# Batch 0 of a fused cosFormer attention and MLP kernel: row sums of k by a selector weight, fewer idle matmuls, another order of chunk 0, two pieces of q on GpSimd

## The chip, the cores and the metric

The kernel runs on one core of a Trainium2 chip. The metric is the device time of one execution in microseconds (us). All times below that carry a decimal point and no other unit are microseconds from the start of the profiled span.

## The reference, cut to what matters

q, k and v are [8 batches, 8 heads, 576 positions, 64], the weights are w_in [512, 2048] and w_out [2048, 512], all float32.

```python
def phi(x, c, s):                       # c, s: cos and sin of pi/2 * position / 576
    r = np.maximum(x, 0.0)
    return np.concatenate([r * c, r * s], axis=-1)      # 64 -> 128 features
q_p, k_p = phi(q, cos_w, sin_w), phi(k, cos_w, sin_w)
kv  = np.einsum('bhsf,bhsd->bhfd', k_p, v)
z   = np.sum(k_p, axis=2)
num = np.einsum('bhsf,bhfd->bhsd', q_p, kv)
den = np.einsum('bhsf,bhf->bhs', q_p, z)[..., None] + 1e-06
x   = (num / den).transpose(0, 2, 1, 3).reshape(8 * 576, 512)
h   = x @ w_in
out = (h * (1.0 / (1.0 + np.exp(-1.702 * h)))) @ w_out
```

## The kernel before, in words

The batches are worked one after the other. Of each batch, the attention part gives x, four chunks of 128 rows and a tail of 64; `mm1` multiplies x by w_in in 16 column blocks (fc) of 128, `gelu` evacuates each block on ScalarE (ACT), and `mm2` multiplies by w_out. The attention work of the next batch is spread between the `mm2` calls of the batch at hand. Batch 0 has no batch before it, so its attention part stands alone at the start, and this is the part that the change touches.

The program is written in a fixed order (`tc.manual_schedule()`): each engine works through its own instructions in the order in which the calls stand in the text, and waits where an operand isn't ready. The tiles of the two PSUM pools (`pmm`, four buffers named mm; `pat`, two buffers named at) are handed out again when the last reader of a buffer is done; a new tile takes the buffer whose release comes first in the program.

Batch 0 goes like this:

- SyncE (SP) loads k and q as float32 in two cuts each. GpSimd (POOL) waits for the first piece of k (`gate`, L141), then issues the two halves of v as bfloat16 (`vb`, L143), then blocks 0 to 3 and 4 to 7 of w_in (`load_win`, L122), and after a second gate that waits for the end of v (L146) the rest of w_in and the loads of batch 1.
- `idle` (L387) gives TensorE (PE) matmuls on zeros until k is there: 12 of 512 columns and 48 of 64.
- `trig` (L156 on ACT, L158 on VectorE, DVE) makes the features of k (`kr`) and q (`qn`), position piece j of 9 at a time, a cosine and a sine instruction each.
- `ksum` (L235) sums k's features over the positions: for each of four head pairs i and nine pieces j a matmul with `kr[:, j, i, :]` as the weight and the two columns of `sel` as the moving operand, 36 in all; a DVE copy (L237) puts them as column 64 into `kvs`.
- `qturn_pe` (L191) transposes q's features, two pieces j at a time, and `qevac` (L201 on DVE, L199 on ACT) copies them to `qT`.
- `kv_mm` (L223) makes k'v for head pairs 0 and 1 from v's first half, then for pairs 2 and 3 from the second; `kv_evac` (L228) copies each to `kvs`.
- `num_halves` (L247 to L257) makes numerator, denominator and quotient of chunk 0 in two halves of four heads; `x_half` (L265, L267) turns each into `xT`. Chunks 1 to 3 take `num_mm` (L274), `num_div` (L282 to L286), `xturn_mm` (L303) and `xturn_evac` (L310, ACT).
- `x_part(c)` (L326) multiplies chunk c by blocks fc 0 to 3 of w_in: 4 fc by 4 pieces kc of the contraction, 16 matmuls of 128 columns. Chunk 0 is cut in two calls (fc 0 and 1, then 2 and 3), and the transposes of chunk 1 stand between them; those of chunk 2 stand ahead of `x_part(1)`, those of chunk 3 ahead of `x_part(2)`.
- `gelu` (L331) then evacuates the four blocks, and `mm1` of fc 4 and later follow with 512 columns each.

Of the kernel before, what the change touches and what calls it, by code (L numbers as in the profile page):

```python
# [9 lines left out]
F32 = mybir.dt.float32  # L10
BF16 = mybir.dt.bfloat16
AF = mybir.ActivationFunctionType
MUL = mybir.AluOpType.mult
ADD = mybir.AluOpType.add
MAX = mybir.AluOpType.max
# [4 lines left out]
def kernel(  # L20
# [9 lines left out]
    nc = tc.nc  # L30
    B, H, S, D = q.shape
    d_model = H * D
    d_ff = moe_w_in.shape[1]
    KC = d_model // 128
    FC = d_ff // 128
    NS = S // 64
    MT = 512
# [7 lines left out]
    small = ctx.enter_context(tc.tile_pool(name="small", bufs=3))  # L45
    pmm = ctx.enter_context(tc.tile_pool(name="pmm", bufs=4, space=PSUM))
# [12 lines left out]
    kf, vf, vb = raw("kf"), raw("vf"), raw("vb", BF16)  # L59
    qf0 = qf[:, 0:NI * S].rearrange("p (i e) -> p i e", i=NI)  # L60
# [10 lines left out]
    ident = const.tile([128, 128], BF16)  # L71
# [3 lines left out]
    warm = const.tile([128, 512], BF16)  # L75
# [10 lines left out]
    sel = const.tile([128, 2], BF16)  # L86
# [9 lines left out]
    kr = one.tile([128, NS, NI, 128], BF16, name="kr")  # L96
# [4 lines left out]
    qT = one.tile([128, H, 640], BF16, name="qT")  # L101
# [18 lines left out]
    def load_win(i, f0):  # L120
        n = w_in_t[i].shape[2]
        nc.gpsimd.dma_start(out=w_in_t[i], in_=win_r[:, :, f0:f0 + n])  # L122

    def wcol(kc, fc):

        g, c = divmod(fc, 4)
        w = w_in_t[g][:, kc, :] if g < 2 else w_in_t[2][:, kc, ts(g - 2, 512)]
        return w.rearrange("p (f c) -> p f c", c=4)[:, :, c]
# [14 lines left out]
        nc.gpsimd.dma_start(out=vb[:, i:i + 2], in_=src_of(v, 0, i, i + 2))  # L143
    load_win(0, 0)
    load_win(1, 512)
    nc.gpsimd.tensor_copy(gate[0:1, 1:2], vb[0:1, 3, 0:1])  # L146
    load_win(2, 1024)


    def trig(dst, src, j, act=False):  # L150

        i = src[:, :, ts(j, 64)]
        for cs, w in enumerate((cosw, sinw)):
            o = dst[:, j, :, ts(cs, 64)]
            if act is True or (act == "sin" and cs == 1):
                nc.scalar.activation(o, i, AF.Relu, scale=w[:, j:j + 1])  # L156
            else:
                nc.vector.tensor_scalar(o, i, 0.0, w[:, j:j + 1], op0=MAX, op1=MUL)  # L158

    def trig_q(c, act=False):  # L160
        n = 128 if c < 4 else 64
# [21 lines left out]
    def qturn_pe(c, at=False):  # L183
        if at:
            tp = pat.tile([128, 2, 512], F32, name="at")[:, 0].bitcast(BF16).rearrange(
                "p (j i t) -> p j i t", j=2, i=NI)
        else:
            tp = pmm.tile([128, 2, NI, 128], BF16, name="mm")
        for j in range(2 * c, min(2 * c + 2, NS)):
            for i in range(NI):  # L190
                nc.tensor.transpose(tp[:, j % 2, i], qn0[:, j, i, :], ident)  # L191
        tps[c] = tp

    def qevac(c, act=False):
        n = min(2 * c + 2, NS) - 2 * c
        o = qT[:, :, ds(c * 128, n * 64)].rearrange("f h (j p) -> f j h p", j=n)
        i = tps[c][:, 0:n].rearrange("f j i (hh p) -> f j (i hh) p", hh=2)
        if act:
            nc.scalar.activation(o, i, AF.Copy)  # L199
        else:  # L200
            nc.vector.tensor_copy(o, i)  # L201
# [6 lines left out]
    st = {}  # L208

    def kv_open(i0=0, i1=NI, n=65):  # L210
        t = pat.tile([128, 2, 512], F32, name="at")
        for i in range(i0, i1):
            st["kv", i] = t[:, :, ds((i - i0) * n, n)]
        st["ps", i0] = t[:, :, 0:(i1 - i0) * n]
        if i0 == 0:
            st["kvs"] = small.tile([128, 2, NI, VW], BF16, name="kvs", bufs=2)

    def kv_mm(i0, i1, rhs, col, n):
        for i in range(i0, i1):
            for j in range(NS):  # L220
                for hh in range(2):
                    r = slice(hh * 64, hh * 64 + 64)
                    nc.tensor.matmul(st["kv", i][:, hh, ds(col, n)], kr[r, j, i, :], rhs(r, i, j),  # L223
                                     start=(j == 0), stop=(j == NS - 1))

    def kv_evac(i0, i1, n=65):
        o = st["kvs"][:, :, i0:i1, 0:n]
        nc.vector.tensor_copy(o, st["ps", i0].rearrange("p hh (i e) -> p hh i e", e=n))  # L228

    def ksum():  # L230

        t = pmm.tile([128, 512], F32, name="mm")
        for i in range(NI):
            for j in range(NS):
                nc.tensor.matmul(t[:, ts(i, 2)], kr[:, j, i, :], sel,  # L235
                                 start=(j == 0), stop=(j == NS - 1))
        nc.vector.tensor_copy(st["kvs"][:, :, :, 64].rearrange("p hh i -> p i hh"),  # L237
                              t[:, 0:8].rearrange("p (i hh) -> p i hh", hh=2))

    nums = {}  # L240


    def num_halves():
        ps = [pmm.tile([128, 512], F32, name="mm") for _ in range(2)]
        for h in range(H):
            i, hh = divmod(h, 2)
            nc.tensor.matmul(ps[h // 4][:, ds((h % 4) * 65, 65)], qT[:, h, 0:128],  # L247
                             st["kvs"][:, hh, i, 0:65], start=True, stop=True)
        pv = [p[:, 0:260].rearrange("p (h e) -> p h e", h=4) for p in ps]
        den = small.tile([128, 2, 4], F32, name="den")  # L250
        for a in range(2):
            nc.vector.tensor_scalar(den[:, a], pv[a][:, :, 64], 1e-6, None, op0=ADD)
        inv = small.tile([128, 2, 4], F32, name="inv")
        nc.vector.reciprocal(inv, den)
        for a in range(2):
            xn = small.tile([128, 4, 64], BF16, name="xh")
            nc.vector.tensor_tensor(xn, pv[a][:, :, 0:64],  # L257
                                    inv[:, a].unsqueeze(2).to_broadcast([128, 4, 64]), op=MUL)
            nums[0, a] = [ps[a], xn]

    def x_half(b, a):
        ps, xn = nums.pop((0, a))
        o = ps[:, 264:392].bitcast(BF16)
        for k in range(2):
            nc.tensor.transpose(o[:, ts(k, 128)], xn.rearrange("p h e -> p (h e)")[:, ts(k, 128)],  # L265
                                ident)
        nc.scalar.activation(x_cols(b, 0)[:, 2 * a:2 * a + 2], o.rearrange("p (k t) -> p k t", k=2),  # L267
                             AF.Copy)
# [9 lines left out]
    def num_div(c):  # L278
        ps = nums[c][0]
        pv = ps[:, :, 0:260].rearrange("p a (h e) -> p a h e", h=4)  # L280
        den = small.tile([128, 2, 4], F32, name="den")
        nc.vector.tensor_scalar(den, pv[:, :, :, 64], 1e-6, None, op0=ADD)  # L282
        inv = small.tile([128, 2, 4], F32, name="inv")
        nc.vector.reciprocal(inv, den)
        xn = small.tile([128, 2, 4, 64], BF16, name="xn", bufs=4)
        nc.vector.tensor_tensor(xn, pv[:, :, :, 0:64],  # L286
                                inv.unsqueeze(3).to_broadcast([128, 2, 4, 64]), op=MUL)
        nums[c].append(xn)
# [3 lines left out]
    def x_open(b):  # L292
        x[b] = xpool.tile([128, KC, MT], BF16, name="xT")
# [4 lines left out]
    def xturn_mm(c):  # L298
        ps, xn = nums[c]
        xv = xn.rearrange("p a h e -> p (a h e)")  # L300
        for kc in range(KC):
            o = ps[:, kc // 2, ds(264 + (kc % 2) * 64, 64)].bitcast(BF16)
            nc.tensor.transpose(o, xv[:, ts(kc, 128)], ident)  # L303
# [80 lines left out]
    def idle(n, cols=512):  # L384
        w = pmm.tile([128, 512], F32, name="mm")
        for _ in range(n):
            nc.tensor.matmul(w[:, 0:cols], warm[:, 0:128], warm[:, 0:cols], start=True, stop=True)  # L387
# [26 lines left out]
        xturn_evac(b, 4)  # L414


    idle(12)
    idle(48, 64)
    for j in (0, 1):
        trig(kr, kf, j)  # L420
    trig(kr, kf, 2, act=True)
# [2 lines left out]
    trig(kr, kf, 6, act="sin")  # L424
    for j in (7, 8):
        trig(kr, kf, j, act=True)
    kv_open(0, 2, 64)
    kv_open(2, 4, 64)
    for j in (0, 1):
        trig(qn0, qf0, j)  # L430
    for j in (2, 3):
        trig(qn0, qf0, j, act=True)
    ksum()
    qturn_pe(0)
    qevac(0)
    qturn_pe(1)
    qevac(1)
    for j in (4, 5, 7):
        trig(qn0, qf0, j, act=True)
    trig(qn0, qf0, 6)  # L440
    kv_mm(0, 2, vb_rhs, 0, 64)
    kv_evac(0, 2, 64)
    qturn_pe(2)
    qevac(2, act=True)
    kv_mm(2, 4, vb_rhs, 0, 64)
    kv_evac(2, 4, 64)
    qturn_pe(3)
    qevac(3, act=True)
    x_open(0)
    num_halves()  # L450
    num_mm(1)
    num_div(1)
    x_half(0, 0)
    x_half(0, 1)
    num_mm(2)
    num_div(2)

    def x_part(c, f0=0, f1=4):
        for fc in range(f0, f1):
            mm1_part(0, fc, c * 128, c * 128 + 128)  # L460

    x_part(0, 0, 2)
    xturn_mm(1)
    xturn_evac(0, 1)
    x_part(0, 2, 4)
    num_mm(3)
    num_div(3)
    xturn_mm(2)
    xturn_evac(0, 2)
    x_part(1)  # L470
    xturn_mm(3)
    xturn_evac(0, 3)
    trig(qn0, qf0, 8)
    x_part(2)
    x_part(3)
    for fc in range(4):
        gelu(fc)
# [144 lines left out]
```

## Time and profile before

| what | value |
|---|---|
| time, median of 3 runs (lowest to highest) | 292.13 us (291.91 to 292.35) |
| the profiled execution: its own time, and its span | 292.35 us, 290.6 us |
| PE busy | 283.8 us, 98% of the span |
| ACT, DVE, POOL busy | 128.0, 124.4, 56.4 us |
| granted TensorE clock | 0.999 |

The span runs from the first to the last instruction; the execution's own time has 1.75 us more around it. "Busy" of PE counts a matmul until its result is in PSUM, so that a stream of short matmuls is busy without a gap while its starts are some 56 ns apart. In the chain of work that ended last each piece stands at the time when it became what everything later waited for; in the timeline each piece stands at its first start.

### The profile page before, as it was taken

What the parts mean: (1) busy time and instruction counts of PE and PEld (TensorE: products, weight loads), DVE (VectorE), ACT (ScalarE), POOL (GpSimd) and SP (SyncE); (2) the same over time, 40 slices, a digit from 0 to 9 for tenths busy, and PEclk for the clock granted to TensorE, in tenths of its full rate; (3) what the DMA queues carried; (4) which work ended last, traced back from release to release, by engine and by line L of the source; (5) the groups of instructions that cost most, each with busy time, mean ns of one, the idle gap of its engine ahead of it and who ended that gap; (6) DMA issues with size and microseconds to landing.
All of it is one profiled execution on the core that took longest, in us unless ns stands there. A gap on an engine that the chain in (4) does not pass through costs nothing.

```text
span 290.6 us, 5918 instructions
## 1 busy us (share of the span) xinstructions
PE 283.8 (98%) x2396; PEld 156.1 (54%) x2396; DVE 124.4 (43%) x360; ACT 128.0 (44%) x223; POOL 56.4 (19%) x60
## 2 busy tenths in 40 slices
PE   8889999999999999999999999999999999999995
PEld 3775646855545554555455545554555455554444
DVE  4856514872695248615950587048804300000000
ACT  6957733662147213641265116601671156751111
POOL 6332003200055013601250016001600100001000
PEclk9999999999999999999999999999999999999999
DMA  7999999999999998897799479958901410002322
GB/s 246 245 219 290 350 167 228 356 243 237 283 282 219 333 187 184 181 379 157 158 202 398 112 149 165 392 167 119 186 13 55 107 68 1 0 2 45 84 88 74
DMA packets 73211, 53.54 MB, mean 184 GB/s; under 512 B 52608, under 2 KB 62592, under 8 KB 73184
## 3 DMA queue, kind: packets, MB, share of 16 engines
q1 hardware_dynamic: 67216, 37.24, 54.7%
q0 software_dynamic: 5968, 15.93, 20.5%
q8 instruction: 19, 0.31, 0.4%
q14 instruction: 8, 0.07, 0.1%
HBM read 36.70 MB, written 9.44 MB: 159 GB/s over the span
## 4 chain that ended last, share of the span: by engine, by line
PE 91%; DMA 6%; DVE 1%; ACT 0%; POOL 0%; issue 0%; ACTq 0%
PE mm L375 41%; PE mm L326 38%; PE mm L354 4%; PE at L223 3%; PE at L274 3%; DMA vb<-in_v_dram 2%; DMA xT<-xn 2%; DMA kf<-in_k_dram 1%; PE mm L347 1%; PE at L303 1%; POOL vb L143 0%; PE mm L191 0%; DVE xn L286 0%; ACT xT L310 0%; PE mm L265 0%
## 5 line engine op out<-in xcount | busy, mean ns | idle before, releaser
L375 PE MATMUL mm<-w_out_sb,g 128*128 128x512 bf16 (+1 forms) x528 | 117.4, 373 | 0.0
L326 PE MATMUL mm<-xT,w_in 128*128 128x512 bf16 (+1 forms) x608 | 114.1, 345 | 0.4 <-ACT xT L267 0.2
L331 ACT ACTIVATE g<-mm 128x512 bf16<-128x512 f32 x128 | 75.6, 598 | 33.0 <-PE mm L326 33.0
L326 PEld LDWEIGHTS <-w_in 128*128 128x128 bf16 x608 | 61.4, 113 | 49.7 <-issue 0.6
L382 POOL DMA_DIRECT2D out_dram<-ysb x34 | 45.5, 1339 | 195.6 <-ACT ysb L379 195.5
L375 PEld LDWEIGHTS <-g 128*128 128x128 bf16 x528 | 48.8, 98 | 50.0
L379 ACT ACTIVATE ysb<-mm 128x512 f32<-128x512 f32 (+1 forms) x37 | 21.7, 586 | 115.6 <-PE mm L375 115.6
L286 DVE TENSOR_TENSOR xn<-at,inv 128x512 bf16<-128x512 f32 x39 | 27.0, 691 | 4.0 <-DMA xT<-xn 2.7
L228 DVE CAST kvs<-at 128x520 bf16<-128x520 f32 (+1 forms) x9 | 5.8, 640 | 53.2 <-PE at L223 53.2
L158 DVE TENSOR_SCALAR kr<-kf,cosw 128x256 bf16<-128x256 f32 x69 | 24.2, 351 | 6.0 <-DMA kf<-in_k_dram 6.0
L158 DVE TENSOR_SCALAR kr<-kf,sinw 128x256 bf16<-128x256 f32 x68 | 23.2, 341 | 0.0
L282 DVE TENSOR_SCALAR den<-at 128x8 f32<-128x8 f32 x39 | 6.5, 166 | 32.1 <-PE at L274 32.1
L274 PEld LDWEIGHTS <-qT 128*128 128x128 bf16 x312 | 14.2, 97 | 7.7 <-issue 0.6
L171 DVE TENSOR_SCALAR qn<-qf,cosw 128x512 bf16<-128x512 f32 (+1 forms) x33 | 15.8, 478 | 3.2 <-DMA qf<-in_q_dram 3.2
L171 DVE TENSOR_SCALAR qn<-qf,sinw 128x512 bf16<-128x512 f32 (+1 forms) x33 | 15.8, 478 | 0.0
L274 PE MATMUL at<-kvs,qT 128*128 128x65 bf16 x312 | 15.5, 193 | 0.2 <-ACT xT L310 0.2
L375 PE MATMUL mm<-w_out_sb,gt 128*128 128x512 bf16 x64 | 14.0, 379 | 0.0
L354 PE MATMUL mm<-xt,w_in 128*128 128x448 bf16 x64 | 12.3, 352 | 0.0
L223 PEld LDWEIGHTS <-kr 64*128 64x128 bf16 x576 | 9.3, 94 | 3.3 <-issue 2.9
L375 PEld LDWEIGHTS <-gt 128*128 128x128 bf16 x64 | 6.3, 98 | 7.5
L356 ACT ACTIVATE gt<-mm 128x448 bf16<-128x448 f32 x16 | 8.7, 544 | 3.3 <-PE mm L354 3.2
L354 PEld LDWEIGHTS <-w_in 128*128 128x128 bf16 x64 | 7.3, 114 | 4.9
(69 smaller groups left out, 99.7 us busy)
## 6 DMA issues: line engine op xcount, KB each, us to landing
kf<-in_k_dram SPq DMA_DIRECT2D x6, 1152.0 KB, 10.3
vf<-in_v_dram SPq DMA_DIRECT2D x6, 1152.0 KB, 11.7
qf<-in_q_dram SPq DMA_DIRECT2D x6, 1024.0 KB, 6.0
out_dram<-ysb POOLq DMA_DIRECT2D x24, 256.0 KB, 4.3
w_out_sb<-in_moe_w_out_dram POOLq DMA_DIRECT2D x4, 512.0 KB, 17.1
out_dram<-ysb POOLq DMA_DIRECT2D x10, 128.0 KB, 7.4
kf<-in_k_dram POOLq DMA_DIRECT2D x1, 1152.0 KB, 13.0
vf<-in_v_dram POOLq DMA_DIRECT2D x1, 1152.0 KB, 15.8
```

Of the source, the lines that this page charges most:

```text
L158: nc.vector.tensor_scalar(o, i, 0.0, w[:, j:j + 1], op0=MAX, op1=MUL)
L171: nc.vector.tensor_scalar(o, i, 0.0, sc, op0=MAX, op1=MUL)
L223: nc.tensor.matmul(st["kv", i][:, hh, ds(col, n)], kr[r, j, i, :], rhs(r, i, j), start=(j == 0), stop=(j == NS - 1))
L274: nc.tensor.matmul(ps[:, h // 4, ds((h % 4) * 65, 65)], qT[:, h, ts(c, 128)], st["kvs"][:, hh, i, 0:65], start=True, stop=True)
L286: nc.vector.tensor_tensor(xn, pv[:, :, :, 0:64], inv.unsqueeze(3).to_broadcast([128, 2, 4, 64]), op=MUL)
L326: nc.tensor.matmul(hp[fc][:, t0:t1], wcol(kc, fc), x[b][:, kc, t0:t1], start=(kc == 0), stop=(kc == KC - 1))
L331: nc.scalar.activation(g, hp.pop(fc), AF.Gelu_apprx_sigmoid)
L354: nc.tensor.matmul(hps[:, 64:B * 64], wcol(kc, fc), xt[:, kc, 64:B * 64], start=(kc == 0), stop=(kc == KC - 1))
L356: nc.scalar.activation(gt[:, fc, 64:B * 64], hps[:, 64:B * 64], AF.Gelu_apprx_sigmoid)
L375: nc.tensor.matmul(yp[b, t, c0][:, c0:c1], w, w_out_sb[:, fc, c0:c1], start=(fc == 0), stop=(fc == FC - 1))
L379: nc.scalar.activation(ysb[:, c0:c1], yp[b, t, c0][:, c0:c1], AF.Identity)
L382: eng.dma_start(out=dst[:, c0:c1], in_=ysb[p0:p0 + n, c0:c1])
```

## The change

- The 60 idle matmuls become 9 of 512 columns. Five more stand between the matmuls of the sums.
- The sums of k take `sel` as the weight and a whole piece `kr[:, j]` (512 columns) as the moving operand: 9 matmuls (`ksum_mm`) into rows 0 and 1 of one tile, in the order in which the pieces become ready. A DVE copy of [2, 512] takes the rows to SBUF (`ksum_rows`), four matmuls against a 2 by 2 identity turn them into columns (`ksum_turn`), and the old DVE copy puts them into `kvs`.
- Pieces 6 and 8 of q go from DVE to GpSimd, ahead of the gate and of the load of the last part of w_in, which move behind them in POOL's queue. Pieces 4, 5 and 7 stay on ACT and move ahead in the text.
- Chunk 0's numerator and quotient for heads 0 to 3 (`num_half(0)`, `div_half(0)`) stand ahead of `kv_mm(2, 4)`, and `x_half(0, 0)` stands between `kv_evac(2, 4)` and `qturn_pe(3)`. The other half follows `qturn_pe(3)`.
- `x_part(0)` is one block of 16 matmuls, the contraction's first two pieces for all four fc, and then the last two. The transposes of chunk 1 stand behind all of it, those of chunk 2 behind `x_part(1)`, and those of chunk 3 behind `x_part(2)`.

```diff
-    nc.gpsimd.tensor_copy(gate[0:1, 1:2], vb[0:1, 3, 0:1])
-    load_win(2, 1024)
...
-    def ksum():
-
-        t = pmm.tile([128, 512], F32, name="mm")
+    def ksum_mm(j, first=False, last=False):
+
+        if first:
+            st["ks"] = pmm.tile([128, 512], F32, name="mm")
+        nc.tensor.matmul(st["ks"][0:2], sel, kr[:, j].rearrange("p i f -> p (i f)"),
+                         start=first, stop=last)
+
+    def ksum_rows():
+        st["row"] = small.tile([2, 512], BF16, name="row", bufs=1)
+        nc.vector.tensor_copy(st["row"], st["ks"][0:2])
+
+    def ksum_turn():
         for i in range(NI):
-            for j in range(NS):
-                nc.tensor.matmul(t[:, ts(i, 2)], kr[:, j, i, :], sel,
-                                 start=(j == 0), stop=(j == NS - 1))
+            nc.tensor.matmul(st["ks"][:, ts(i, 2)], st["row"][:, ts(i, 128)], ident[0:2, 0:2],
+                             start=True, stop=True)
...
-    idle(12)
-    idle(48, 64)
+    idle(9)
...
+    for n, j in ((0, 0), (0, 2), (0, 1), (4, 3), (0, 7), (1, 4), (1, 8), (0, 5), (0, 6)):
+        if n:
+            for _ in range(n):
+                nc.tensor.matmul(spare, warm[:, 0:128], warm, start=True, stop=True)
+        ksum_mm(j, first=(j == 0), last=(j == 6))
+        if j == 0:
+            spare = pmm.tile([128, 512], F32, name="mm")
     kv_open(0, 2, 64)
     kv_open(2, 4, 64)
     for j in (0, 1):
         trig(qn0, qf0, j)
-    for j in (2, 3):
+    for j in (2, 3, 4, 5, 7):
         trig(qn0, qf0, j, act=True)
-    ksum()
+    for j in (6, 8):
+        trig(qn0, qf0, j, eng=nc.gpsimd)
+    nc.gpsimd.tensor_copy(gate[0:1, 1:2], vb[0:1, 3, 0:1])
+    load_win(2, 1024)
+    ksum_rows()
     qturn_pe(0)
     qevac(0)
     qturn_pe(1)
     qevac(1)
-    for j in (4, 5, 7):
-        trig(qn0, qf0, j, act=True)
-    trig(qn0, qf0, 6)
+    ksum_turn()
     kv_mm(0, 2, vb_rhs, 0, 64)
     kv_evac(0, 2, 64)
     qturn_pe(2)
     qevac(2, act=True)
+    num_half_open()
+    num_half(0)
+    div_half(0)
+    x_open(0)
     kv_mm(2, 4, vb_rhs, 0, 64)
     kv_evac(2, 4, 64)
+    x_half(0, 0)
     qturn_pe(3)
     qevac(3, act=True)
-    x_open(0)
-    num_halves()
+    num_half(1)
+    div_half(1)
     num_mm(1)
     num_div(1)
-    x_half(0, 0)
     x_half(0, 1)
     num_mm(2)
     num_div(2)
...
-    x_part(0, 0, 2)
+    for fc in (0, 1, 3, 2):
+        hp[fc] = pmm.tile([128, MT], F32, name="mm")
+    for k0 in (0, 2):
+        for fc in range(4):
+            for kc in (k0, k0 + 1):
+                nc.tensor.matmul(hp[fc][:, 0:128], wcol(kc, fc), x[0][:, kc, 0:128],
+                                 start=(kc == 0), stop=(kc == KC - 1))
     xturn_mm(1)
     xturn_evac(0, 1)
-    x_part(0, 2, 4)
     num_mm(3)
     num_div(3)
+    x_part(1)
     xturn_mm(2)
     xturn_evac(0, 2)
-    x_part(1)
+    x_part(2)
     xturn_mm(3)
     xturn_evac(0, 3)
-    trig(qn0, qf0, 8)
-    x_part(2)
     x_part(3)
```

`num_half(a)` and `div_half(a)` do for half a what `num_halves` did for both, with a reciprocal of four columns for each half.

More of the change, by code (lines that the diff above doesn't have):

```diff
@@ L145, with trig @@
     load_win(1, 512)
-    nc.gpsimd.tensor_copy(gate[0:1, 1:2], vb[0:1, 3, 0:1])
-    load_win(2, 1024)
-    def trig(dst, src, j, act=False):
+    def trig(dst, src, j, act=False, eng=nc.vector):
         i = src[:, :, ts(j, 64)]
@@ L157, in trig @@
             else:
-                nc.vector.tensor_scalar(o, i, 0.0, w[:, j:j + 1], op0=MAX, op1=MUL)
+                eng.tensor_scalar(o, i, 0.0, w[:, j:j + 1], op0=MAX, op1=MUL)
     def trig_q(c, act=False):
@@ L233, in ksum @@
+    def ksum_turn():
         for i in range(NI):
-            for j in range(NS):
-                nc.tensor.matmul(t[:, ts(i, 2)], kr[:, j, i, :], sel,
-                                 start=(j == 0), stop=(j == NS - 1))
+            nc.tensor.matmul(st["ks"][:, ts(i, 2)], st["row"][:, ts(i, 128)], ident[0:2, 0:2],
+                             start=True, stop=True)
         nc.vector.tensor_copy(st["kvs"][:, :, :, 64].rearrange("p hh i -> p i hh"),
-                              t[:, 0:8].rearrange("p (i hh) -> p i hh", hh=2))
+                              st["ks"][:, 0:8].rearrange("p (i hh) -> p i hh", hh=2))
@@ L240, with num_half_open, num_half @@
     nums = {}
-    def num_halves():
-        ps = [pmm.tile([128, 512], F32, name="mm") for _ in range(2)]
-        for h in range(H):
+    def num_half_open():
+        nums["ps"] = [pmm.tile([128, 512], F32, name="mm") for _ in range(2)]
+    def num_half(a):
+        ps = nums["ps"][a]
+        for h in range(4 * a, 4 * a + 4):
             i, hh = divmod(h, 2)
-            nc.tensor.matmul(ps[h // 4][:, ds((h % 4) * 65, 65)], qT[:, h, 0:128],
+            nc.tensor.matmul(ps[:, ds((h % 4) * 65, 65)], qT[:, h, 0:128],
@@ L248, in num_halves, with div_half @@
                              st["kvs"][:, hh, i, 0:65], start=True, stop=True)
[L249 to L253, printed above, removed]
-        nc.vector.reciprocal(inv, den)
[L255 to L259, printed above, removed]
+    def div_half(a):
+        pv = nums["ps"][a][:, 0:260].rearrange("p (h e) -> p h e", h=4)
+        den = small.tile([128, 4], F32, name="denh")
+        nc.vector.tensor_scalar(den, pv[:, :, 64], 1e-6, None, op0=ADD)
+        inv = small.tile([128, 4], F32, name="invh")
+        nc.vector.reciprocal(inv, den)
+        xn = small.tile([128, 4, 64], BF16, name="xh")
+        nc.vector.tensor_tensor(xn, pv[:, :, 0:64],
+                                inv.unsqueeze(2).to_broadcast([128, 4, 64]), op=MUL)
+        nums[0, a] = [nums["ps"][a], xn]
@@ L456, with x_part @@
     num_div(2)
-    def x_part(c, f0=0, f1=4):
-        for fc in range(f0, f1):
+    def x_part(c):
+        for fc in range(4):
             mm1_part(0, fc, c * 128, c * 128 + 128)
-    x_part(0, 0, 2)
+    for fc in (0, 1, 3, 2):
+        hp[fc] = pmm.tile([128, MT], F32, name="mm")
+    for k0 in (0, 2):
+        for fc in range(4):
+            for kc in (k0, k0 + 1):
+                nc.tensor.matmul(hp[fc][:, 0:128], wcol(kc, fc), x[0][:, kc, 0:128],
+                                 start=(kc == 0), stop=(kc == KC - 1))
     xturn_mm(1)
     xturn_evac(0, 1)
-    x_part(0, 2, 4)
     num_mm(3)
     num_div(3)
+    x_part(1)
     xturn_mm(2)
     xturn_evac(0, 2)
-    x_part(1)
+    x_part(2)
     xturn_mm(3)
     xturn_evac(0, 3)
-    trig(qn0, qf0, 8)
-    x_part(2)
     x_part(3)
```

## The prediction

> **What bounds the kernel now.** First the page's list of engines and its slices: PE is busy nearly always, at full clock.
>
> ```profile
> PE 283.8 (98%) x2396; PEld 156.1 (54%) x2396; DVE 124.4 (43%) x360; ACT 128.0 (44%) x223; POOL 56.4 (19%) x60
> PE   8889999999999999999999999999999999999995
> PEclk9999999999999999999999999999999999999999
> ```
>
> Next the waits of PE over the whole span (engine, line, what it waited for, us in total, times, longest). All but the last line lie before 17.4:
>
> ```profile
> PE mm L387 <- DVE warm L76: 1.3, 1, 1.3
> PE mm L265 <- DVE xh L257: 0.7, 1, 0.7
> PE mm L235 <- DVE kr L158: 0.5, 2, 0.3
> PE at L274 <- ACT xT L310: 0.2, 1, 0.2
> PE mm L326 <- ACT xT L267: 0.2, 1, 0.2
> PE mm L326 <- DMA xT<-xn: 0.2, 1, 0.2
> ```
>
> So what moves the first matmul of `x_part(3)` moves the end by as much; later waits can give back 0.2 at most. Then the chain that ended last (start, us, what) shows who sets that time:
>
> ```profile
> 5.39 6.84 DMA vb<-in_v_dram
> ...
> 15.77 0.64 PE mm L326 x8
> 16.41 0.24 PE at L303 x4
> 16.65 0.02 issue
> 16.67 0.61 ACT xT L310
> 17.28 0.04 issue
> 17.32 0.41 PE at L274 x8
> ...
> 18.94 0.40 PE at L303 x4
> 19.34 1.79 PE mm L326 x32
> 21.13 0.01 issue
> 21.14 1.02 PE mm L326 x4
> ```
>
> v's second half lands at 12.23; the copy of chunk 1's transposes (0.61) is waited for in full. Last the timeline of weight loads and matmuls, with first starts and, in brackets, idle time and releaser:
>
> ```profile
> 15.77 0.48 PEld L326 LDWEIGHTS <-w_in 128*128 128x128 bf16 x8 [0.31 <-DMA w_in<-in_moe_w_in_dram]
> 16.25 0.39 PE L303 MATMUL at<-ident,xn 128*128 128x128 bf16 x4
> 17.32 0.40 PE L274 MATMUL at<-kvs,qT 128*128 128x65 bf16 x8 [0.24 <-ACT xT L310]
> 17.78 1.06 PE L326 MATMUL mm<-xT,w_in 128*128 128x128 bf16 x16
> 19.18 2.99 PE L326 MATMUL mm<-xT,w_in 128*128 128x128 bf16 x36
> ```
>
> The first line decides much: `x_part(0)` starts at 15.77 because the first part of w_in has just landed (issued at 6.12, 9.6 to landing: 15.72). The weights of its first matmuls wait for no other thing, so nothing done earlier makes chunk 0 start sooner. In lines two and three, from the first transpose of chunk 1 (16.25) to the first matmul that needs its copy (17.32) 1.07 pass: 0.42 to ACT's start, 0.61 copy, 0.04 back to PE. Of this the transposes' own issue is 0.23; 0.85 is open and has to be covered. Before, two fc of `x_part(0)` cover 0.45 of it, and the copies of chunks 2 and 3 lie wholly beside `x_part(1)` and `x_part(2)`.
>
> **The change, part by part.** All times are those of the profiled execution (292.35 own time, 290.6 span; 0.22 above the median of 292.13).
>
> *Start and idle matmuls.* PE is idle until 1.26; 12 matmuls of 512 columns then start 0.425 apart until 6.35, and the 48 of 64 columns 34 ns apart. Nine end at 1.26 + 9 x 0.427 = 5.10; pieces 0, 2 and 1 of k are ready at 5.05, 5.32 and 5.75 (ends of L158 and L156) and take 0.43 each, to 6.39, so PE stays busy as before until the fast rate begins. At that rate (0.216 for 512 columns, from 6.91 for 32) the sums follow the pieces: the last piece (6, DVE, ends 8.81) leaves 5 and 6 to do, end about 9.2. Before, the 36 small matmuls ended at 9.84. This gains nothing by itself: q's piece 1 is ready at 9.86.
>
> *Rows.* The copy [2, 512] costs DVE about what 128x520 costs it in L228 (0.64); bounds 0.42 (128x256) and 0.69 (L201). It stands between q's last piece (9.86) and `qevac(0)`, so `qevac(0)` and `qevac(1)` end near 11.65 as before. Four small matmuls and the old copy (0.19) follow. Piece 6 (11.56 to 12.16 on DVE) is gone, so `kv_evac(0,2)` runs at 11.72 instead of 12.08 and ends at 12.14.
>
> *First half ahead of v's second half.* `num_half(0)` starts at 12.19 and takes 0.12 (half of 0.24 for eight): `kv_mm(2,4)` starts at 12.31 instead of 12.27. It costs nearly nothing, since PE waited for v there. But DVE now has `div_half(0)` ahead of `kv_evac(2,4)`: denominator 12.52, reciprocal 12.72, quotient 12.95 to 13.37 (steps 0.20, 0.23, 0.42 from L282 to L257), so `kv_evac(2,4)` ends at 13.71 instead of 13.43. Then on PE: `x_half(0,0)` 13.42, `qturn_pe(3)` 13.55, `num_half(1)` 14.00, `num_mm(1)` 14.12, `x_half(0,1)` 15.23 (after its quotient, 15.18), `num_mm(2)` 15.36 to 15.60. ACT: `qevac(3)` 14.20 to 15.22, copy of the second half 15.55 to 15.93 (15.76 before). All before w_in or just behind: PE is at `x_part(0)` 0.17 early, the second half is needed at 16.22 and is 0.28 early, chunk 1's quotient (16.27) 0.40 early. The gain goes into the wait for w_in.
>
> *GpSimd.* No row shows this operation. The nearest are the 128x512 memset (0.53, half of it 0.27) and the 128x128 select (0.29, twice it 0.59); I take 0.5 for an instruction and keep 0.27 to 1.5 for the range. q's second cut lands at 9.60 (2.40 + 7.2), so piece 6 is ready at 10.6, needed at 13.77: no cost up to 2.0 each. The gate and w_in's last part (12.41 before, after v at 12.23) come behind four of them, 11.6: not later; even 3 us later they would be behind w_in's second part in the same queue (landed 18.3, and the last 23.3; first used after 25). Loads of batch 1 behind them lose what cover allows, and q's of batch 1 may start earlier than 19.98. No PE wait hangs on it.
>
> Three of DVE's instructions on k took 0.53, 0.66 and 0.56 instead of 0.34 while POOL was issuing DMAs (4.96, 6.37, 7.20), so the two can hold each other up by 0.3. Here they meet only from 9.60 to 9.86: taken as nothing. The Trainium skill's "SBUF — State Buffer", section "Who interferes with whom", says that VectorE in a two-port mode and GpSimd exclude each other for a whole instruction; by it q's piece 1 could be 0.35 late, and the sum 0.1 more.
>
> *The order of the x parts.* Here the change costs. Matmuls of 128 columns come 1.79/32 = 0.056 apart, 16 take 0.894. Before: 15.77 to the first matmul of `x_part(3)` at 19.18 + 0.894 = 20.07. After: `x_part(0)` 15.77 to 16.67; transposes of chunk 1 at 16.67, and now nothing covers their copy, since `num_mm(3)` needs the buffer it frees and `x_part(1)` its result: 16.67 + 1.08 = 17.75. `num_mm(3)` 0.23, `x_part(1)` to 18.87. Transposes of chunk 2, and directly behind them `x_part(2)`, which needs them: 19.95 to 20.85. Chunk 3 likewise: `x_part(3)` starts at 21.93. That is 1.86 later. As a check: work 64 x 0.056 + 4 x 0.23 = 4.50 in both; uncovered 0.66 before (0.40 at 16.92, 0.26 at 18.68), 3 x 0.85 = 2.55 after; the difference is 1.89.
>
> Moving piece 8 of q off DVE (0.6 at 18.80) is worth nothing: PE needs it at 22.
>
> Sum: +1.86. Own time 292.35 + 1.86 = 294.2; against the median, 292.13 + 1.86 = 294.0.
>
> **The rivals.**
>
> *Not slower: PE doesn't run in the order of the text.* If the transposes of chunks 2 and 3 went ahead of `x_part(1)` and `x_part(2)`, as their inputs (17.26 and 19.32) nearly allow, the two copies would be covered: `num_mm(3)` 17.75, transposes 17.98, `x_part(1)` 18.21, transposes 19.32, `x_part(2)` 19.55, `x_part(3)` 20.45: +0.38, 292.5. With chunk 1's transposes ahead of the end of `x_part(0)` as well it is -0.07, and only with w_in 0.6 earlier on top it would be faster. It decides at the first matmul behind the transposes of chunk 2. Against it: before, every group on PE from 7.9 to 24 stands as in the text. 0.06, and 0.03 for faster.
>
> *The early part comes late.* If PE's fast rate begins one pause later, near 9.8 instead of 6.35, the sums end at 10.7 instead of 9.2, `num_half(0)` is 1.0 late, 0.28 of it hidden: +0.7 on the sum, 294.7. For it: fewer idle matmuls and less load in each; against: PE has no gap up to 7.25. The Trainium skill's "TensorE: Matmul & The Clock Gate", Part 1, has the gate open only after a full busy window of about 3.4 us that runs freely, so one window missed is what this would be; this trace, with a start at 1.26 and the change at 6.35, does not exclude it. 0.08.
>
> *GpSimd is the bound.* At 3 us an instruction piece 6 is ready at 15.65, `qturn_pe(3)` ends 2.1 late, and 1.9 reach the end: 295.9. No POOL compute row is near that. 0.03.
>
> **How the numbers follow.** The forecast itself has 0.80, at 294.0. Its own bounds: if a bare copy costs the 0.67 of the chain's view (16.65 to 17.32) instead of 0.85, it is 0.54 less, and 0.2 may be given back later: 293.2. The upper end takes in the late start with 0.3 for slow GpSimd pieces or contention: 295.0. What ran before spreads over 0.44; about 0.2%, 0.58, can be told from no change. Slower: 0.80 + 0.08 + 0.03 = 0.91; same 0.06; faster 0.03.
>
> **What would show it.** Right: the weights of the first L326 group released by w_in near 15.7; three gaps on PE, each released by ACT's xT copy, about 0.85 between starts, ahead of `num_mm(3)`, `x_part(2)` and `x_part(3)`; gelu's first start near 22.35 instead of 20.49; after it the same chain, shifted. Wrong: chunk 0 starting well before 15.7, the copies covered, a wait for `qn` at L191, or a PE wait later that is gone.

## The result, and the profile after

The changed kernel takes 293.29 us (median of 18 runs, 293.17 to 293.88); the kernel before, run beside it, 291.92 (18 runs, 291.56 to 294.37). The ratio is 1.0037, with a 95% interval of 1.0022 to 1.0051: slower by 0.6 to 1.5 us, where 1.86 (a ratio of 1.0064) was forecast. The ratio agrees with that of the means (293.33 and 292.26); the medians are 1.37 apart, the lowest times 1.61. The means are the closest because the kernel before has some long runs: of its 76 runs beside the experiments, for which the clock is on record, 13 have a granted clock of 0.993 to 0.994 and take 292.76 to 295.47, while none of the changed kernel's 18 is below 0.999.

The profiled execution has 293.88 as its own time and a span of 292.2. PE's waits of the changed kernel (engine, line, what it waited for, us in total, times, longest):

```profile
PE mm L335 <- ACT xT L319: 1.4, 2, 0.7
PE mm L396 <- DVE warm L76: 1.2, 1, 1.2
PE mm L274 <- DVE xh L266: 1.0, 2, 0.7
PE at L283 <- ACT xT L319: 0.7, 1, 0.7
PE at L221 <- DMA vb<-in_v_dram: 0.6, 1, 0.6
```

There are three waits of 0.7 for the copy to `xT`, and no wait for a DMA transpose (`xT<-xn`) any more. The timeline of PE in the changed kernel, with first starts (L488 is `x_part(0)`, L312 the transposes, L283 `num_mm(3)`, L335 the other x parts):

```profile
15.98 1.11 PE L488 MATMUL mm<-xT,w_in 128*128 128x128 bf16 x16
16.92 0.39 PE L312 MATMUL at<-ident,xn 128*128 128x128 bf16 x4
18.00 0.40 PE L283 MATMUL at<-kvs,qT 128*128 128x65 bf16 x8 [0.69 <-ACT xT L319]
18.23 1.06 PE L335 MATMUL mm<-xT,w_in 128*128 128x128 bf16 x16
19.13 0.39 PE L312 MATMUL at<-ident,xn 128*128 128x128 bf16 x4
20.20 1.05 PE L335 MATMUL mm<-xT,w_in 128*128 128x128 bf16 x16 [0.69 <-ACT xT L319]
21.09 0.39 PE L312 MATMUL at<-ident,xn 128*128 128x128 bf16 x4
22.17 2.09 PE L335 MATMUL mm<-xT,w_in 128*128 128x128 bf16 x19 [0.69 <-ACT xT L319]
```

From the transposes to what needs them pass 1.08, 1.07 and 1.08, as worked out. `x_part(3)` starts 6.19 after `x_part(0)`; the forecast had 6.16.

One relation orders all that follows. An execution's own time less the first start of `x_part(3)` (20.07 before, 22.17 after; where it stands in one group with `x_part(2)`, that group's first start + 0.894) is 271.71 to 271.75 in the changed kernel and in the eight of the experiments e1, e3, e4, g1, g3, g4, k1 and k2. It is 272.28 in the kernel before, 272.21 in e2 and 272.45 in g2, and these three are those whose PE rows show a wait for `xT<-xn`. So a time has two parts that vary in these twelve executions: when `x_part(3)` starts, and what batches 2 and 3 lose to their DMA transposes. By this, and if its median run has no such loss, the changed kernel's median has `x_part(3)` at 293.29 - 271.72 = 21.57 and `x_part(0)` at 15.38. These two are estimates: the one profiled execution was its slowest, v having landed some 0.5 late.

### The profile page after: what moved, and what is told of

It is laid out like the page before. It is cut to its first block, busy times and chain, and to the rows that moved or that the text cites. A ratio compares the mean times of both kernels' runs of the same rounds, so it can differ in the third digit from the quotient of the medians.

```text
span 292.2 us, 5752 instructions
## 1 busy us (share of the span) xinstructions
PE 281.6 (96%) x2295; PEld 154.2 (53%) x2328; DVE 124.0 (42%) x358; ACT 128.3 (44%) x223; POOL 58.3 (20%) x64
## 4 chain that ended last, share of the span: by engine, by line
PE 91%; DMA 4%; ACT 2%; issue 1%; DVE 1%; ACTq 0%; POOL 0%
PE mm L384 42%; PE mm L335 36%; PE mm L363 4%; PE at L283 3%; PE at L221 3%; DMA vb<-in_v_dram 2%; ACT g L340 1%; DMA kf<-in_k_dram 1%; PE mm L356 1%; PE at L312 1%; ACT xT L319 1%; PE mm L189 0%; PE mm L488 0%; DVE xh L266 0%; DVE xn L295 0%
## 5 line engine op out<-in xcount | busy, mean ns | idle before, releaser
L384 PE MATMUL mm<-w_out_sb,g 128*128 128x512 bf16 (+1 forms) x507 | 115.7, 372 | 1.4 <-issue 0.3
L335 PE MATMUL mm<-xT,w_in 128*128 128x512 bf16 (+1 forms) x582 | 112.3, 348 | 1.9 <-ACT xT L319 1.4
L335 PEld LDWEIGHTS <-w_in 128*128 128x128 bf16 x592 | 60.8, 113 | 50.3 <-issue 1.6
L391 POOL DMA_DIRECT2D out_dram<-ysb x34 | 42.8, 1259 | 198.8 <-ACT ysb L388 198.7
L156 DVE TENSOR_SCALAR kr<-kf,cosw 128x256 bf16<-128x256 f32 x69 | 23.6, 343 | 3.2 <-DMA kf<-in_k_dram 3.2
L156 DVE TENSOR_SCALAR kr<-kf,sinw 128x256 bf16<-128x256 f32 x68 | 23.5, 345 | 0.0
L283 PEld LDWEIGHTS <-qT 128*128 128x128 bf16 x312 | 14.2, 97 | 8.1 <-issue 0.8
L169 DVE TENSOR_SCALAR qn<-qf,cosw 128x512 bf16<-128x512 f32 (+1 forms) x33 | 15.8, 477 | 3.1 <-DMA qf<-in_q_dram 3.1
L283 PE MATMUL at<-kvs,qT 128*128 128x65 bf16 x312 | 15.5, 193 | 0.7 <-ACT xT L319 0.7
L169 DVE TENSOR_SCALAR qn<-qf,sinw 128x512 bf16<-128x512 f32 (+1 forms) x33 | 15.8, 478 | 0.0
## 6 DMA issues: line engine op xcount, KB each, us to landing
vf<-in_v_dram SPq DMA_DIRECT2D x6, 1152.0 KB, 11.2
```

What stands on the lines that cost most here:

```text
L156: eng.tensor_scalar(o, i, 0.0, w[:, j:j + 1], op0=MAX, op1=MUL)
L169: nc.vector.tensor_scalar(o, i, 0.0, sc, op0=MAX, op1=MUL)
L283: nc.tensor.matmul(ps[:, h // 4, ds((h % 4) * 65, 65)], qT[:, h, ts(c, 128)], st["kvs"][:, hh, i, 0:65], start=True, stop=True)
L335: nc.tensor.matmul(hp[fc][:, t0:t1], wcol(kc, fc), x[b][:, kc, t0:t1], start=(kc == 0), stop=(kc == KC - 1))
L384: nc.tensor.matmul(yp[b, t, c0][:, c0:c1], w, w_out_sb[:, fc, c0:c1], start=(fc == 0), stop=(fc == FC - 1))
L391: eng.dma_start(out=dst[:, c0:c1], in_=ysb[p0:p0 + n, c0:c1])
```

## The experiments

Theory A: the uncovered copies are the loss, and what stands ahead of `x_part(0)` brings nothing. Rivals: B, the early part gains and the order loses all; C, the early part itself is late. Theory D came after the first four runs.

Each result is a median with its lowest and highest time, then the ratio to the kernel before with its 95% interval. The kernel before ran beside e1 to e4 (median 291.82, lowest 291.52), beside g1 to g4 (291.91, 291.53) and beside k1 and k2 (292.01, 291.58). The changed kernel ran in a set of its own (before: 291.92, 291.56), so a difference to it is one between sets.

**e1: the old order of the x parts in the changed kernel.**

```diff
-    for k0 in (0, 2):
...
+    x_part(0, 0, 2)
     xturn_mm(1)
     xturn_evac(0, 1)
+    x_part(0, 2, 4)
     num_mm(3)
     num_div(3)
-    x_part(1)
     xturn_mm(2)
     xturn_evac(0, 2)
-    x_part(2)
+    x_part(1)
     xturn_mm(3)
     xturn_evac(0, 3)
+    x_part(2)
     x_part(3)
```

> The changed kernel with the old order of the x parts only: x_part(0) in two calls with the transposes of chunk 1 between them, those of chunks 2 and 3 ahead of x_part(1) and x_part(2). Theory A (the uncovered copies are the loss, and what stands ahead of x_part(0) brings and costs nothing, since x_part(0) waits for w_in): within 0.3 of the kernel before, the first matmul of x_part(3) near 20.1, no gap of 0.85 behind the transposes. Theory B (the early part gains 0.5 to 0.8, and the order loses the full 1.9): 0.5 to 0.8 faster than before, x_part(0) starting near 15.1. Theory C (the early part itself is late, by GpSimd or by v): 0.5 or more slower than before.

291.93 (291.55 to 292.75) beside 291.82 (291.52 to 294.06); ratio 0.9993 (0.9976 to 1.0010). The loss is gone with the order, and with the old order the early part is worth nothing: A, not B or C. A's reason, a wait for w_in, does not hold: no such wait is left. `x_part(0)` started at 15.65, but its third matmul only at 16.04, when the copy of the second half was done (at 15.99; in the kernel before at 15.75). So the transposes of chunk 1 start at 16.38 (16.25 before).

**e2: the new order alone, in the kernel before.**

```diff
-    x_part(0, 0, 2)
+    for k0 in (0, 2):
...
     xturn_mm(1)
     xturn_evac(0, 1)
-    x_part(0, 2, 4)
     num_mm(3)
     num_div(3)
+    x_part(1)
     xturn_mm(2)
     xturn_evac(0, 2)
-    x_part(1)
+    x_part(2)
     xturn_mm(3)
     xturn_evac(0, 3)
     trig(qn0, qf0, 8)
-    x_part(2)
     x_part(3)
```

> The kernel before with the new order of the x parts only (piece 8 of q stays on VectorE, behind the copy of chunk 3). Theory A: three gaps of about 0.85 between starts, x_part(3) 1.86 later than in the kernel before (near 21.9), and the end 1.3 to 1.4 later, since some 0.5 is taken back at later waits for the DMA transposes of batches 2 and 3. Theory B: the end 1.9 later. Theory C: under 0.7 later.

293.94 (293.31 to 296.38), ratio 1.0062 (1.0038 to 1.0086), that is +1.8; the medians are 2.12 apart, the lowest times 1.79. `x_part(3)` started at 21.96, 1.89 later than before, and what follows took as long (272.21, before 272.28). The forecast's term for the order stands, and it reaches the end: nothing like 0.5 is taken back. With the same order, the changed kernel is 0.65 faster than this one by the medians but 0.14 by the lowest times. A part of the 0.65 is later waits (0.49 in e2's profiled execution), so what the early part brings can't be read from this alone.

**e3: a delay of known size.** Nine idle matmuls of 512 columns ahead of `x_part(3)` in the kernel before:

```diff
+    slow = pat.tile([128, 2, 512], F32, name="at")
+    for _ in range(9):
+        nc.tensor.matmul(slow[:, 0], warm[:, 0:128], warm, start=True, stop=True)
     x_part(3)
```

> The kernel before with nine idle matmuls of 512 columns ahead of x_part(3), 9 x 0.216 = 1.94 of PE time and nothing else. Theory A (part of any delay of PE at this place is taken back later): the end 1.4 to 1.5 later, and the waits for xT at the first mm1 of batches 2 and 3 shorter. Theory B (PE is the bound without slack from here on): 1.9 later.

293.62 (293.44 to 296.26), ratio 1.0064 (1.0042 to 1.0085): +1.87 of 1.94, and 1.92 between the lowest times. PE is the bound from here on, as the forecast had it; that a delay is partly given back, my reading after the first comparison, fell. (The interval, 1.2 to 2.5, would leave room for it; the lowest times do not, nor does the rest behind `x_part(3)`, 271.72 here, as in the kernels without a delay that show no wait for `xT<-xn`.) What looked like it in the two profiles (2.10 at `x_part(3)`, 1.53 at the end) is a wait that one execution had and the other had not.

**e4: pieces 6 and 8 of q back on VectorE**, with the gate and w_in's last part at their old place.

```diff
-    for j in (6, 8):
-        trig(qn0, qf0, j, eng=nc.gpsimd)
...
     ksum_turn()
+    trig(qn0, qf0, 6)
     kv_mm(0, 2, vb_rhs, 0, 64)
```

> The changed kernel with pieces 6 and 8 of q back on VectorE (6 ahead of kv_evac(0,2), 8 behind the copy of chunk 3) and the gate and the load of w_in's last part back at their old place. Theory A: as the changed kernel within 0.3 (the pieces lie beside other work), at most 0.2 slower through kv_evac(0,2), 0.5 later. Theory C (GpSimd's pieces or the late loads cost): 0.5 or more faster than the changed kernel.

293.88 (293.78 to 294.17; one of nine runs, 500.28, aside), ratio 1.0062 (1.0042 to 1.0083): 0.59 slower than the changed kernel by the medians, 0.61 by the lowest times. VectorE in e4:

```profile
11.49 0.17 DVE L243 CAST kvs<-mm 128x8 bf16<-128x8 f32 x1
11.56 0.33 DVE L156 TENSOR_SCALAR qn<-qf,cosw 128x256 bf16<-128x256 f32 x1
11.82 0.33 DVE L156 TENSOR_SCALAR qn<-qf,sinw 128x256 bf16<-128x256 f32 x1
12.08 0.41 DVE L226 CAST kvs<-at 128x256 bf16<-128x256 f32 x1
```

The two instructions stand right ahead of `kv_evac(0,2)`, for which `num_half(0)` and behind it `kv_mm(2,4)` wait: 12.76 instead of 12.30 to 12.35 where v was on time (g2, k2, g4). `x_part(0)` starts at 15.90 instead of 15.50 (g4), which is 0.40 of the 0.59. On GpSimd an instruction takes 1.13 to 1.14, not 0.5, and it still costs nothing. C fell, and so did A's 0.3: piece 6 does not lie beside other work.

This left a question: the early part gains in the new order, though `x_part(0)` was to wait for w_in until 15.7 in any case. In e1 and e4 w_in's first part landed at 14.6 and 14.7 (6.0 + 8.6 and 6.1 + 8.6, issue and time to landing), in before, e2 and e3 at 15.5 to 15.8. One more thing moves with it: a packet of instructions, 16 KB, that one of the 16 DMA engines loads (PE's, as far as g2 shows: there only matmuls were added, and it moved). The DMA queues of the kernel before, from 12.5 to 13.0 (packets, MB, share of 16 engines):

```profile
q8 instruction: 1, 0.02, 12.2%
```

12.2% of 16 engines' 0.5 us are 0.98 us of one engine. In the kernels with 14 idle matmuls instead of 60 this packet comes at 14.5 to 15.5. Theory D: it holds w_in's first part up.

**g1: sums as rows and few idle matmuls only**, in the kernel before; the nine `ksum_mm` and their idle matmuls stand where the changed kernel has them, `ksum_turn` behind `qevac(1)`.

```diff
-    idle(12)
-    idle(48, 64)
+    idle(9)
...
-    ksum()
+    ksum_rows()
```

> The kernel before with k's sums as rows and nine idle matmuls (five more between the sums) only: 69 matmuls fewer at the start, pieces of q, halves and x parts as before. Theory D (the packet of instructions that one DMA engine loads at 12.5 in the kernels with 60 idle matmuls, and at 15.0 in those with 14, holds w_in's first part up by about 1): the packet comes after 13.5, w_in's first part lands at 14.6 to 15.0 instead of 15.5 to 15.8; the end is within 0.3 of the kernel before, since x_part(0) then waits for the copy of the second half (15.76). Theory E (w_in lands earlier for another part of the change, or by chance): it lands at 15.5 or later.

291.72 (291.47 to 292.37) beside 291.91; ratio 0.9989 (0.9974 to 1.0004). The packet comes at 14.5 and w_in's first part lands at 14.5 (5.9 + 8.6). The load with its time to landing, first in the kernel before, then in g1:

```profile
w_in<-in_moe_w_in_dram POOLq DMA_DIRECT2D x1, 512.0 KB, 9.6
w_in<-in_moe_w_in_dram POOLq DMA_DIRECT2D x1, 512.0 KB, 8.6
```

PE no longer waits for it:

```profile
15.18 0.26 PEld L334 LDWEIGHTS <-w_in 128*128 128x128 bf16 x3
15.60 0.34 PEld L334 LDWEIGHTS <-w_in 128*128 128x128 bf16 x5 [0.16 <-issue]
```

**g2: 48 more matmuls in the same PE time**, in the changed kernel: four idle matmuls of 512 columns at the start become 32 of 64, four between the sums become 24 of 64.

```diff
-    idle(9)
+    idle(5)
+    idle(32, 64)
...
+            m, cols = (24, 64) if n == 4 else (n, 512)
```

> The changed kernel with 48 more PE matmuls in the same PE time: four idle matmuls of 512 columns at the start become 32 of 64, and the four between the sums become 24 of 64. Theory D: the packet of instructions comes back to 12 to 13.3, w_in's first part lands at 15.5 to 15.8, x_part(0) starts then, and the end is 0.2 to 0.4 later than in the changed kernel. Theory E: w_in lands by 15.0 as in e1 and e4, the end as in the changed kernel within 0.1.

294.35 (four runs, 294.19 to 294.54), ratio 1.0080 (1.0060 to 1.0100), 1.06 slower than the changed kernel. The packet is back at 13.0, w_in's first part lands at 15.74 (6.04 + 9.7), and the weights of `x_part(0)` wait again:

```profile
15.74 0.93 PEld L490 LDWEIGHTS <-w_in 128*128 128x128 bf16 x16 [0.27 <-DMA w_in<-in_moe_w_in_dram]
```

That is the 0.3 expected. The other 0.7 is a wait of batch 2 for its DMA transposes (27.42 from one `kv_mm` to the next, 71.56 to 98.98, instead of 26.68), which was not expected; all four runs are high enough to have it. The 48 matmuls move both. With v on time, the four kernels with the packet at 12.5 to 13.5 (before, e2, e3, g2) have w_in at 15.5 to 15.8, and the five with it at 14.5 or later (e1, e4, g1, g4, k2) at 14.5 to 14.8: D holds that far, with one profiled execution of each. Where v landed late (the changed kernel, g3, k1) w_in landed at 15.35 to 15.6, though the packet came at 15.0 or later. That it is the packet itself that holds up the load was not isolated.

**g3: both halves of chunk 0 behind `kv_mm(2,4)` again**, in the changed kernel.

```diff
-    num_half_open()
-    num_half(0)
-    div_half(0)
-    x_open(0)
     kv_mm(2, 4, vb_rhs, 0, 64)
     kv_evac(2, 4, 64)
-    x_half(0, 0)
     qturn_pe(3)
     qevac(3, act=True)
+    num_half_open()
+    num_half(0)
+    div_half(0)
+    x_open(0)
     num_half(1)
     div_half(1)
     num_mm(1)
     num_div(1)
+    x_half(0, 0)
     x_half(0, 1)
```

> The changed kernel with both halves of chunk 0 behind kv_mm(2,4) and qturn_pe(3) again, in the order of the kernel before, the rest as changed. Theory A: v's second part starts on PE at 12.27 instead of some 12.35, but chunk 0's quotients both come behind it: x_part(0) 0.1 to 0.3 later, the end 0.1 to 0.3 later than in the changed kernel. If putting the half ahead costs instead (VectorE has it ahead of kv_evac(2,4)), the end is 0.1 to 0.3 earlier.

293.75 (five runs, 293.55 to 294.33), ratio 1.0062 (1.0044 to 1.0081): 0.46 slower than the changed kernel by the medians, 0.38 by the lowest times, more than the 0.1 to 0.3 expected. Putting the half ahead gains. Its one profile has v 0.9 late, so where the gain sits in it, and how much of it is v, can't be read.

**g4: only chunk 1's copy uncovered**, in the changed kernel.

```diff
+    xturn_mm(2)
+    xturn_evac(0, 2)
     x_part(1)
-    xturn_mm(2)
-    xturn_evac(0, 2)
+    xturn_mm(3)
+    xturn_evac(0, 3)
     x_part(2)
-    xturn_mm(3)
-    xturn_evac(0, 3)
     x_part(3)
```

> The changed kernel with the transposes of chunk 2 ahead of x_part(1) and those of chunk 3 ahead of x_part(2) again; x_part(0) stays one block, with the copy of chunk 1 uncovered. Theory A (each uncovered copy costs 0.85 of PE's starts): two gaps go, 1.70 less, and the wait for chunk 3's quotient (0.26) comes back: 1.4 to 1.5 earlier than the changed kernel, the lowest time near 291.7. If the chain's 0.67 for each is what a copy costs: 1.1 earlier.

292.03 (291.69 to 293.12), ratio 1.0004 (0.9991 to 1.0016): 1.26 earlier than the changed kernel by the medians, 1.48 by the lowest. From `x_part(0)` to `x_part(3)`, 15.50 to 19.37 + 0.894, are 4.76 instead of 6.19, so the 0.85 for a copy is the right price. PE in g4:

```profile
15.50 1.11 PE L488 MATMUL mm<-xT,w_in 128*128 128x128 bf16 x16
16.44 0.39 PE L312 MATMUL at<-ident,xn 128*128 128x128 bf16 x4
17.51 0.40 PE L283 MATMUL at<-kvs,qT 128*128 128x65 bf16 x8 [0.69 <-ACT xT L319]
17.75 0.39 PE L312 MATMUL at<-ident,xn 128*128 128x128 bf16 x4
17.97 1.06 PE L335 MATMUL mm<-xT,w_in 128*128 128x128 bf16 x16
19.14 0.40 PE L312 MATMUL at<-ident,xn 128*128 128x128 bf16 x4
19.37 2.99 PE L335 MATMUL mm<-xT,w_in 128*128 128x128 bf16 x35
```

**k1 and k2: versions that might beat both.** g1 and e1 with `x_part(0)` cut by the contraction, pieces kc 0 and 1 of all four fc (`x_first(0)`) and then 2 and 3:

```diff
-    x_part(0, 0, 2)
+    x_first(0)
     xturn_mm(1)
     xturn_evac(0, 1)
-    x_part(0, 2, 4)
+    x_first(2)
```

> A version that might beat both: the kernel before with k's sums as rows and few idle matmuls (g1), and x_part(0) cut by the contraction instead of by fc: its first two pieces for all four fc, the transposes of chunk 1, then the last two pieces. If the copy of the second half holds x_part(0) (15.26 to 15.7 in g1), the transposes of chunk 1 start up to 0.3 earlier and the end with them; if the quotient of chunk 1 on VectorE does (ready near 15.85), 0.1 or less: 0 to 0.1 faster than g1, 0.1 to 0.4 faster than before.

> The changed kernel with the old order of the transposes and x_part(0) cut by the contraction as in k1. If the early part of the change is worth something once w_in has landed early and no copy is uncovered, it shows here: 0.2 or more faster than e1. If VectorE's quotient of chunk 1 (near 16.3 in e1) sets the transposes, as e1 within 0.1, and not faster than k1.

k1: 291.59 (291.43 to 292.49) beside 292.01 (291.58 to 295.47), ratio 0.9970 (0.9945 to 0.9996); k2: 291.74 (291.55 to 292.42), ratio 0.9978 (0.9959 to 0.9998). Both beat the changed kernel by 1.5 to 1.7. Against the kernel before the lowest times differ by 0.15 and 0.03 only, so that the gain is mostly that they have fewer long runs; why they have fewer was not tested. k2 starts the transposes of chunk 1 at 16.14 (e1: 16.38), but its lowest time is that of e1 and it is not faster than k1.

## Why the prediction was right or wrong

The direction and the mechanism were right: three uncovered copies at 0.85 each, from an order that PE keeps. e1, e2, e3 and g4 bear out the term (1.8 where 1.86 was worked out), its price and that it reaches the end undiminished. The size of the whole was wrong: 1.86 against 0.6 to 1.5. The lowest times are 1.61 apart, 0.25 less than forecast. The means come another 0.54 closer, because the runs of the kernel before lie 0.70 above its lowest on average and those of the changed kernel only 0.16. Against the time forecast, the relation above splits the 0.71 between 294.0 and 293.29, as an estimate.

*The step that failed first* is "nothing done earlier makes chunk 0 start sooner", with "the gain goes into the wait for w_in". It took the landing of w_in, 15.72, as fixed, since no DMA ahead of it was moved. With fewer matmuls at the start, as in the changed kernel, it came about 1.0 earlier (14.5 to 14.8 in the five kernels with v on time; g1 and g2 show that it goes with the start's matmuls). Then what I had priced at nothing decides: the half ahead (0.46, g3) and piece 6 off VectorE (0.59, e4). By the estimate `x_part(0)` starts at 15.38 instead of 15.77, and `x_part(3)` at 21.57 instead of 21.93: 0.36 of the 0.71. The profile of g4, the same program up to there, has `x_part(0)` at 15.50. The working ahead of that step was sound: it had PE ready for `x_part(0)` at 15.60, and then let it wait for w_in. A chunk 0 that starts well before 15.7 was named as a sign of being wrong, and so was a later wait of PE that is gone, which is the second step.

*The second* is "later waits can give back 0.2 at most". The row of PE's waits showed 0.2 for `xT<-xn`, but the profiled execution of before had lost 272.28 - 271.72 = 0.56 to it. The rest stood in the chain of the kernel before as matmuls that take longer:

```profile
82.61 14.00 PE mm L326 x64
113.11 13.98 PE mm L326 x64
143.41 13.81 PE mm L326 x64
```

64 matmuls take 13.81 undisturbed; the other two stretches hide 0.19 and 0.17 (with the 0.17 ahead of 113.11, that is 0.53). The median that I added to, 292.13, is 0.34 above an execution without such waits (20.07 + 271.72 = 291.79); the changed kernel's 18 runs, 15 of them within 0.22 of the lowest, leave little room for them. That is the other 0.35, of which 0.21 is that three runs gave 292.13 where 18 gave 291.92. A delay of PE does not decide it: e2 has the wait (272.21) and e3 has not (271.72), and both are delayed. Why some executions have it and others not stays open; g2, with four long runs, shows that matmuls at the start bear on it.

*The other steps.* The copy of the rows took 0.68 (0.64 was taken). GpSimd took 1.13 for an instruction, within the range kept and twice the value taken; piece 6 was ready at 12.40, needed near 13.5, and w_in's last part, issued at 14.73 instead of 12.41, cost nothing. GpSimd's first instruction on q began at 10.13, after VectorE's last one at 9.53, so the hold-up between the two that was weighed did not arise. VectorE's reciprocals and quotients took the steps that were added up. Of the rivals, PE kept the order of the text in every run, the fast rate of PE came in time (the four idle matmuls behind the sums start 0.216 apart in the changed kernel, at 6.03), and GpSimd was not the bound. gelu first started at 22.59, with v late; 22.35 was forecast.

## What to carry to other kernels

Where PE hands a tile to another engine and takes it back, the price of leaving that trip uncovered is the time between starts (here 1.08, of which 0.23 is PE's own), and it counts once for each trip; work that does not need the copy belongs between, before anything is gained upstream. A transfer that bounds a stage is not fixed because no transfer was moved: ask what else its DMA engines carry, and look at the landing again in a run. And before adding a difference to a measured time, find the waits that this time already holds, which a modelled busy row can hide; a sum such as "own time less the start of the last disturbed stage", compared over several kernels, shows them.

## What the runs showed of the hardware that was not expected

- A packet of instructions (16 KB) takes 0.9 to 1.0 us of one DMA engine (11.2% to 12.2% of 16 engines in 0.5 us). With v on time, w_in's first part landed about 1 us later where the packet came at 12.5 to 13.5 than where it came at 14.5 or later; that the one causes the other was not isolated.
- Idle matmuls have a cost as instructions, not only as time: 48 more in the same PE time (g2) cost some 0.3 us at `x_part(0)` and 1.06 at the end.
- The same work on 128x256, a relu times a factor for each row, takes 1.13 us on GpSimd, 0.34 on VectorE and 0.49 on ACT (changed kernel, L156 and L154).
- In the profiled executions of the changed kernel, g3 and k1, each the slowest of its kernel's runs, v landed 0.5 to 0.9 later than in the other kernels, and `x_part(0)` came later with it (15.98 in the changed kernel, 15.50 in g4).
